# Pairing neighbouring heads, and issuing attention's small fp32 products four in a row on TensorE

## Chip, cores and metric

One core of one Trainium2 chip runs the kernel. The metric is device time in microseconds of one execution. Times of the kernel before are the median of 3 runs and one further execution taken with the profiler.

## What is computed

Attention over `q`, `k`, `v` of 4 batches, 8 heads, 576 positions and 64 features, then two feed-forward layers over the 2304 tokens of 512 features:

```python
q_d, k_d, v_d = (x.reshape(B, H, S // 4, 4, D).mean(axis=3) for x in (q, k, v))
out_d = softmax_attention(q_d, k_d, v_d)          # 144 x 144 scores for each batch and head
out_up = np.repeat(out_d, 4, axis=2)
mask = np.abs(pos[:, None] - pos[None, :]) < 4    # 7 keys for each query
out_local = masked_softmax_attention(q, k, v, mask)
x = (out_up + out_local).transpose(0, 2, 1, 3).reshape(B * S, H * D)
h = x @ w_in                                      # 512 -> 2048
x = (np.maximum(h, 0) + alpha * np.minimum(h, 0)) @ w_out
xn = x / rms(x) * rms_g
g, val = xn @ w_gate, xn @ w_val                  # 512 -> 1536 each
out = (silu(g) * val) @ w_out2
```

## The kernel before, in words

**Dense layers.** Activations and weights are split into a high and a low fp16 half, and each product is three fp16 matmuls (high by high, high by low, low by high). `h_mm` (L1249, tile `hps`) is the product with `w_in`, `o_mm` (L1266, tiles `acc`) that with `w_out`; `m2` holds the second layer: `gps` (L1348) for gate and value, `oacc` (L1377, L1395) for the output. Six blocks of 384 tokens pass through; the first ones run in pieces of 192. The weights arrive as 64-bit words of which `Piece.decode` (L1016) makes fp32 with ScalarE and VectorE; `split` (L345) makes the two halves, one instruction on ScalarE and one on VectorE.

**Attention.** Heads are worked in pairs, as `j` = 0 and 1, that lie on partitions 0 to 63 and 64 to 127. Before, the pair is (h, h+4), so row 64j+d of the tile that goes into the dense layer holds feature d of head h+4j, and `cols` (L967) fetches `w_in` in that order: two transfers of 64 partitions for each half of a piece.

- The pooled attention is `down_tasks` (L561) for batches 1 to 3, and `Dense.down` (L758) for batch 0. For each of 4 pairs it makes 4 fp32 products for the scores (`sps`, L612 and L774) and 4 for the output (`avps`, L651 and L810). A score product takes 64 rows of the array, an output product 64 of its columns, and `j` says which half.
- The local attention of batch 0 is done on TensorE (`Dense.local`, L819) in three chunks `c` of 192 queries and two lanes of two pairs. For each lane and chunk `s1` makes scores (`lsps`): for every pair, half chunk and `j` one mask product (L832, bf16, 102 columns), at the edges of the sequence a product of 3 columns (L835, L837), and the fp32 product of q and k (L839) on top. `s4` makes the output (`lops`, L893), 4 fp32 products for each pair.
- The local attention of batches 1 to 3 (`local_tasks`, L433) runs on GpSimd and VectorE, with (pair, chunk of the sequence) on 128 partitions: partition 32h+c before.

Each fp32 product stands as two records in the trace.

**What sets the order.** At the end `issue_order` (L24) lists all instructions with a table of costs and lags and plays a list scheduler forwards and backwards for 20 rounds; the best order of each engine is written into the program as dependencies. Every engine, the queue of transfers on SP among them, then works in that order. Before, the table charges TensorE at half rate for the first 150 us (`COLD`).

Of the kernel before, what the change touches and what calls it, by code (L numbers as in the profile page):

```python
# [23 lines left out]
def issue_order(tc, nc, rounds=20):  # L24
# [53 lines left out]
    def transfer(o, i):  # L78
        sides = [[c for _, c in a.ap if c > 1] or [1] for a in (o, i)]
        rings = max(x for x in range(1, 17) if not any(s[0] % x for s in sides))  # L80
        n = max(runs(a)[0] for a in (o, i))
        each = 4.0 * min(runs(a)[1] for a in (o, i))
        share = n / 16 * (12.0 + 0.072 * each)
        return max(share, n / rings * (9.0 + 0.042 * each)), max(share, 600.0)

    def cost(k, ins, outs):
# [16 lines left out]
        if e == "DVE":  # L103
            if i.opcode == "Reciprocal":
                return 69 + 6.25 * n
            fast = i.opcode in ("TensorScalarPtr", "TensorCopy") and not any(psum(a) for a in ins)
            fast = fast and len([a for a in ins if free(a) > 1]) < 2
            return 69 + n / (1.92 if fast else 0.96) + 60 * (extra > 0)
# [65 lines left out]
    succs = [[] for _ in count]  # L174
    for k in count:
# [13 lines left out]
    COLD = 150e3  # L189

    def run(P, S, prio, fwd, d):
# [4 lines left out]
        port = 0.0  # L196
        for k in count:
            if not left[k]:
                heapq.heappush(soon[eng[k]], (0.0, k))
        for _ in count:  # L200
# [5 lines left out]
            if fwd and e == "PE" and t <= COLD:  # L206
                real[k] = 2 * d[k] - 2.5
# [27 lines left out]
def kernel(  # L235
# [14 lines left out]
    nc = tc.nc  # L250
# [21 lines left out]
    P_X, P_W, P_H = 13, 14, 15  # L272
    P_N, P_U = 10, 44
# [75 lines left out]
    def setup():  # L349
# [7 lines left out]
        nc.vector.tensor_scalar(out=pidx, in0=pidx, scalar1=NC - 1, scalar2=None, op0=ALU.bitwise_and)  # L357
        nc.vector.tensor_scalar(out=edge[:, 0:1], in0=pidx, scalar1=0, scalar2=NEG, op0=ALU.is_equal, op1=ALU.mult)
        nc.vector.tensor_scalar(out=edge[:, 1:2], in0=pidx, scalar1=NC - 1, scalar2=NEG, op0=ALU.is_equal, op1=ALU.mult)
# [22 lines left out]
    def load_q(g, tag=None):  # L382
# [3 lines left out]
                      ap=[[TT * D, 128], [HP * HS, 2], [1, T * D]])  # L386
# [3 lines left out]
    def load_kv(x, g, tag=None):  # L390
# [5 lines left out]
        def src(p0, n, j0, nj, r0=0, nr=R):  # L396
            return bass.AP(tensor=x.tensor, offset=base + p0 * TT * D + j0 * HP * HS + r0 * D,
                           ap=[[TT * D, n], [HP * HS, nj], [1, nr * D]])

        if b == 0 and t0 == 0:  # L400
            nc.gpsimd.memset(t[0:1, 0, 0:W], 0.0)
            nc.sync.dma_start(out=t[1:113], in_=src(1, 112, 0, 2))
            nc.sync.dma_start(out=t[113:128], in_=src(113, 15, 0, 2))
            nc.sync.dma_start(out=t[0:1, 1:2], in_=src(0, 1, 1, 1))
            nc.sync.dma_start(out=t[0:1, 0:1, W:R], in_=src(0, 1, 0, 1, W, R - W))
        elif b == B - 1 and t0 + T == TT:
            nc.gpsimd.memset(t[96:128, 1, R - W:R], 0.0)
            nc.sync.dma_start(out=t[0:112], in_=src(0, 112, 0, 2))
            nc.sync.dma_start(out=t[112:127], in_=src(112, 15, 0, 2))
            nc.sync.dma_start(out=t[127:128, 0:1], in_=src(127, 1, 0, 1))  # L410
            nc.sync.dma_start(out=t[127:128, 1:2, 0:R - W], in_=src(127, 1, 1, 1, 0, R - W))
        else:
            nc.sync.dma_start(out=t, in_=src(0, 128, 0, 2))
        return t

    def load_sd(x, b, h, tag=None):
        t = rawtile([SH, 2, 2, 4 * D], tag, "sd")
        for j in range(2):
            src = bass.AP(tensor=x.tensor, offset=x.offset + (b * H + h + HP * j) * HS,
# [13 lines left out]
    def local_tasks(g, engs, tags=(None, None, None), av_pool=True, o_at=None):  # L433
# [92 lines left out]
        def trans(half):  # L526
            def f():
# [5 lines left out]
                ps = ps.rearrange("p t (h c r) -> p t h c r", h=HP, r=2)  # L533
# [27 lines left out]
    def down_tasks(b, h, tags=(None, None, None), solo=False):  # L561
# [44 lines left out]
        def smm():  # L606
# [3 lines left out]
            for a in range(2):  # L610
                for j in range(2):
                    nc.tensor.matmul(  # L612
                        ps[j][0:SH, a], t[j * 64:j * 64 + 64, 0, a * SH:(a + 1) * SH],
                        t[j * 64:j * 64 + 64, 1, :], start=True, stop=True)
# [30 lines left out]
        def avm():  # L645
# [3 lines left out]
            for kh in range(2):  # L649
                for j in range(2):  # L650
                    nc.tensor.matmul(ps[j * 64:j * 64 + 64, :], st["pv"][:, kh, j],  # L651
                                     st["aT"][:, j, kh * SD:(kh + 1) * SD], start=(kh == 0), stop=(kh == 1))
# [20 lines left out]
    class Dense:  # L673
# [12 lines left out]
        def load(self, h):  # L686
# [4 lines left out]
            for i, (nm, x) in enumerate((("q", q), ("k", k))):  # L691
                st[nm] = t[0:TP6, i * n:(i + 1) * n]
                for j in range(2):
                    nc.sync.dma_start(
                        out=st[nm].rearrange("p (r j d) -> p r j d", r=R6, j=2)[:, :, j],
                        in_=bass.AP(tensor=x.tensor, offset=x.offset + (self.b * H + h + HP * j) * HS,
                                    ap=[[R6 * D, TP6], [D, R6], [1, D]]))

        def loadv(self, h):
# [4 lines left out]
                in_=bass.AP(tensor=v.tensor, offset=v.offset + (self.b * H + h) * HS,  # L704
                            ap=[[8 * D, SH], [HP * HS, 2], [1, 8 * D]]))

        def vwin(self, h, c):
# [3 lines left out]
            def part(p0, p1, w, nw, j):  # L711
                src = v.offset + (self.b * H + h + HP * j) * HS + (w * QT - W + p0) * D
# [45 lines left out]
        def down(self, h):  # L758
            st = self.st[h]

            def smm():
# [10 lines left out]
                for a in range(2):  # L772
                    for j in range(2):
                        nc.tensor.matmul(  # L774
                            ps[j][0:SH, a], t[j * 64:j * 64 + 64, 0, a * SH:(a + 1) * SH],
                            t[j * 64:j * 64 + 64, 1, :], start=True, stop=True)
# [29 lines left out]
            def avm():  # L806
                ps = ps_t.tile([128, SD], F32, tag="at", name="avps")
                for kh in range(2):
                    for j in range(2):
                        nc.tensor.matmul(ps[j * 64:j * 64 + 64, :], st["pv"][:, j, kh],  # L810
# [798 lines left out]
```

## Time and profile before

| | |
|---|---|
| runs | 1036.86, 1039.5 and 1041.29 us, median 1039.5 |
| profiled execution | 1034.7 us, span 1033.0 us |
| busy, of the span | TensorE 95%, VectorE 68%, ScalarE 49%, GpSimd 14% |
| mean granted TensorE clock | 0.99 |
| chain that ended last | TensorE 73%, VectorE 10%, ScalarE 8%, transfers 5% |

Busy TensorE counts every matmul from its start to its modelled end, and neighbours overlap, so it says that something is under way and not how fast. What a product takes of TensorE is read from the start of one instruction to the start of the next. The clock column knows only what the records of the clock tell; the first of them is at 122.6 us, and until then the column reads 1.00.

### The profile page before, as it was taken

Reading aid. Unit: us, or ns where it says so; the run is one execution under the profiler, and the core shown is the slowest. Engines: PE = TensorE matmul, PEld = TensorE weight load, DVE = VectorE, ACT = ScalarE, POOL = GpSimd, SP = SyncE. Lnnn points to the kernel's source line nnn. Section 1 sums busy time; section 2 is a strip of 40 time slices with the busy share of each in tenths; the row PEclk is TensorE's granted clock in tenths of the full one; section 3 lists DMA queues with packets and bytes.
Section 4 is the critical chain, followed back from the end, with each engine's and each line's share of the span. In section 5 each row is a group of like instructions: output and inputs, shape, how many; then the busy total and the mean of one; then the engine's idle time right before and its main releaser. Section 6 shows DMA issues by size and latency. Waiting matters only on the chain.

```text
span 1033.0 us, 16284 instructions
## 1 busy us (share of the span) xinstructions
PE 977.2 (95%) x6232; PEld 611.1 (59%) x6232; DVE 699.2 (68%) x1483; ACT 506.1 (49%) x1214; POOL 142.1 (14%) x118
## 2 busy tenths in 40 slices
PE   3699989999989999998999999999999999999998
PEld 2465667778966555555666565555556666555554
DVE  1568797899999977999976599994333353352333
ACT  2886898799987465123366532222132242321222
POOL 2422121111201101333200232310000000000000
PEclk9999979999999999999999999999999999999999
DMA  9974543554432133112121021100010000000100
GB/s 173 193 173 142 177 142 101 177 182 140 161 93 92 41 101 105 57 66 70 33 85 60 31 77 47 31 16 16 1 31 2 1 1 1 1 1 1 31 1 31
DMA packets 50008, 74.54 MB, mean 72 GB/s; under 512 B 17718, under 2 KB 30922, under 8 KB 49930
## 3 DMA queue, kind: packets, MB, share of 16 engines
q1 hardware_dynamic: 49930, 73.50, 24.7%
q8 instruction: 49, 0.80, 0.3%
q14 instruction: 29, 0.24, 0.1%
HBM read 68.76 MB, written 4.72 MB: 71 GB/s over the span
## 4 chain that ended last, share of the span: by engine, by line
PE 73%; DVE 10%; ACT 8%; DMA 5%; issue 2%; SPq 1%; POOL 0%; ACTq 0%; DVEq 0%
PE gps L1348 24%; PE hps L1256 15%; PE acc L1269 13%; PE oacc L1377 12%; DMA out_dram<-ob 3%; PE avps L651 2%; ACT sqs L1039 1%; PE lops L893 1%; ACT wr L1020 1%; PE sps L612 1%; DVE ls L460 1%; DVE prod L449 1%; DMA wr<-in_moe_w_in_dram 1%; PE lsps L839 1%; ACT wr L1023 1%
## 5 line engine op out<-in xcount | busy, mean ns | idle before, releaser
L1256 PE MATMUL hps<-xt,wi 128*128 128x192 f16 (+1 forms) x1536 | 359.9, 296 | 4.1 <-DVE g L347 2.8
L1348 PE MATMUL gps<-x,w 128*128 128x384 f16 x1728 | 344.3, 327 | 3.4 <-DVE uhl L1369 1.3
L1269 PE MATMUL acc<-ghl,wo 128*128 128x384 f16 (+1 forms) x960 | 251.6, 311 | 5.4 <-ACT ghl L346 2.7
L1348 PEld LDWEIGHTS <-w 128*128 128x128 f16 x1728 | 169.2, 98 | 117.4 <-issue 6.5
L1377 PE MATMUL oacc<-w,uhl 128*128 128x512 f16 x630 | 192.9, 379 | 1.4 <-ACT ob L1433 1.4
L1256 PEld LDWEIGHTS <-wi 128*128 128x128 f16 x1536 | 153.5, 103 | 68.0 <-issue 16.4
L1269 PEld LDWEIGHTS <-wo 128*128 128x128 f16 x1344 | 128.6, 98 | 69.4 <-issue 8.6
L1262 DVE SCALAR_TENSOR_TENSOR hps<-g,oma,hps 128x192 f32<-128x192 f32 (+1 forms) x128 | 66.1, 517 | 77.9 <-ACT g L1260 77.6
L1357 ACT ACTIVATE th<-gps,tsc 128x384 f32<-128x384 f32 x72 | 41.7, 579 | 143.5 <-PE gps L1348 143.2
L1377 PEld LDWEIGHTS <-uhl 128*128 128x128 f16 x630 | 61.7, 98 | 66.2 <-issue 2.4
L1359 DVE SCALAR_TENSOR_TENSOR th<-th,gps 128x384 f32<-128x384 f32 x72 | 39.6, 550 | 88.4 <-ACT th L1357 88.2
L1260 ACT ACTIVATE g<-hps 128x384 f32<-128x384 f32 x96 | 46.9, 489 | 106.7 <-PE hps L1256 106.6
L1368 ACT ACTIVATE uhl<-gps 128x384 f16<-128x384 f32 x72 | 41.6, 577 | 99.1 <-DVE gps L1362 92.8
L449 POOL TENSOR_TENSOR prod<-cq,ckv 128x896 f32<-128x896 f32 x24 | 52.6, 2194 | 250.3 <-DMA ckv<-in_k_dram 74.2
L1269 PE MATMUL acc<-g,wo 128*128 128x384 f16 (+1 forms) x384 | 67.6, 286 | 1.5 <-ACT x L1283 1.1
L497 POOL TENSOR_TENSOR prod<-ls,ckv 128x896 f32<-128x896 f32 x24 | 45.0, 1875 | 160.8 <-DVE lo L510 60.7
L1369 DVE TENSOR_TENSOR uhl<-gps,uhl 128x384 f16<-128x384 f32 x72 | 45.3, 629 | 30.6 <-ACT uhl L1368 30.4
L510 DVE TENSOR_TENSOR prod<-prod 128x384 f32<-128x384 f32 (+1 forms) x108 | 59.7, 563 | 5.4 <-POOL prod L497 5.4
L346 ACT ACTIVATE ghl<-hps,sc 128x384 f16<-128x384 f32 x72 | 41.7, 579 | 44.2 <-DVE hps L1262 38.4
L347 DVE SCALAR_TENSOR_TENSOR ghl<-hps,sc,ghl 128x384 f16<-128x384 f32 x72 | 44.2, 614 | 25.4 <-ACT ghl L346 25.1
L460 DVE TENSOR_REDUCE ls<-prod 128x14 f32<-128x896 f32 x54 | 57.6, 1075 | 0.0
L1020 ACT ACTIVATE wr<-wr 128x768 f32<-128x768 f32 (+1 forms) x48 | 41.5, 865 | 1.7 <-DMA wr<-in_moe_w_in_dram 1.7
(235 smaller groups left out, 1232.0 us busy)
## 6 DMA issues: line engine op xcount, KB each, us to landing
wr<-in_moe_w_out_dram SPq DMA_DIRECT2D x18, 512.0 KB
wr<-in_moe_w_in_dram SPq DMA_DIRECT2D x20, 384.0 KB
wr<-in_moe_w_gate_dram SPq DMA_DIRECT2D x8, 768.0 KB
wr<-in_moe_w_val_dram SPq DMA_DIRECT2D x8, 768.0 KB
ckv<-in_k_dram SPq DMA_DIRECT2D x7, 768.0 KB
ckv<-in_v_dram SPq DMA_DIRECT2D x7, 768.0 KB
wr<-in_moe_w_out_dram SPq DMA_DIRECT2D x20, 256.0 KB
out_dram<-ob SPq DMA_DIRECT2D x13, 256.0 KB
```

The costliest lines, as they stand in the source:

```text
L449: engs[i].tensor_tensor(out=pr, in0=view(st["q"][:, j, t:t + TP], [[D, TP], [0, ND], [1, D]]), in1=view(st["k"][:, j, t:t + TP], [[D, TP], ...
L460: nc.vector.tensor_reduce(out=st["s"][:, j, t:t + TP], in_=st.pop(("p", i)), axis=AX.X, op=ALU.add)
L497: engs[i].tensor_tensor(out=pr, in0=view(st["s"][:, j, t:t + TP], [[ND, TP], [1, ND], [0, D]]), in1=view(st["v"][:, j, t:t + TP], [[D, TP] ...
L510: add = lambda o, a, c: nc.vector.tensor_tensor(out=o, in0=a, in1=c, op=ALU.add)
L1020: nc.scalar.activation(out=hi.bitcast(F32), in_=hi.bitcast(F32), func=AF.Prelu, scale=2.0 ** -112, alpha=2.0 ** 32)
L1256: nc.tensor.matmul(ps[:, j], wi[:, f + j, a, kk * 128:(kk + 1) * 128], x[:, b_, kk, c0:c0 + n], start=(i == 0), stop=(i == 3 * KK - 1))
L1260: nc.scalar.activation(out=g, in_=ps, func=AF.Relu, scale=-1.0)
L1262: nc.vector.scalar_tensor_tensor(out=ps[:, j], in0=g[:, j], scalar=oma[:, f + j:f + j + 1], in1=ps[:, j], op0=ALU.mult, op1=ALU.add)
L1269: nc.tensor.matmul(acc[e], wo_f(f)[:, a, e * 128:(e + 1) * 128], hl[:, b_], start=(f == 0 and i == 0), stop=(f == NF - 1 and i == 2))
L1348: nc.tensor.matmul(ps, w2_t[i0 + f // 3].rearrange("p a (k c) -> p a k c", k=KK)[:, a, kk, (f % 3) * 128:(f % 3 + 1) * 128], xh[:, b_, kk] ...
L1369: nc.vector.tensor_tensor(out=t1, in0=vp, in1=t0, op=ALU.subtract)
L1377: nc.tensor.matmul(acc[tt], t[:, a, tt * 128:(tt + 1) * 128], w[:, b_, f % 3], start=(f in first and i == 0), stop=(f in last and i == 2))
```

## The change

Heads are paired (2h, 2h+1). Row 64j+d is then feature 128h+64j+d, as `w_in` has it, and a half piece of `w_in` is one transfer to 128 partitions. All loads of `q`, `k` and `v` take the new heads, and the local attention of batches 1 to 3 has partition 4c+h. `load_kv` loses a branch that batch 0 had and cuts its last tile into five transfers in place of four.

In `s1` the mask is written for a whole bank by one product of 408 columns, the edges by products of 2x3, and the fp32 products follow. The four fp32 products of a pair (in `sps`, `avps`, `lsps` and `lops`) are recorded as a group by `together()`. `issue_order` makes the members of a group a chain, lets the first wait for what any of them needs, and puts them on TensorE directly behind each other. Its costs are other ones, and TensorE's rate is now modelled from the work of each stretch.

```diff
-def issue_order(tc, nc, rounds=20):
+def issue_order(tc, nc, groups, rounds=20):
...
-        share = n / 16 * (12.0 + 0.072 * each)
+        share = n / 16 * (10.0 + 0.046 * each)
...
-            if o.ap[0][1] == 64 and o.offset // row(o) == 64:
-                return 22.5
...
-            return n * 2 / 2.4 + 25 if i.is_transpose else n * 4 / 2.4 + 60
+            return n * 2 / 2.4 + 4 if i.is_transpose else n * 4 / 2.4 + 100
...
-                return 69 + 6.25 * n
+                return 89 + 6.25 * n
...
+    mate, joined, fixed = {}, set(), [0.0] * len(insts)
+    for names in groups:
+        g = [at[n] for n in names]
+        for a, b in zip(g, g[1:]):
+            mate[a] = b
+            preds[b].add(a)
+        for a in g:
+            preds[g[0]] |= preds[a].difference(g)
+        joined.update(g)
+        fixed[g[0]] += 100.0
+        fixed[g[-1]] += 145.0
+    for k in joined:
+        dur[k] = free(aps[k][1][0]) * 2 / 2.4 + 2.5
...
-            if fwd and e == "PE" and t <= COLD:
-                real[k] = 2 * d[k] - 2.5
+            if fwd and e == "PE":
+                while t >= (win + 1) * WIN:
+                    slow, win, done = done < BUSY, win + 1, 0
+                done += work[k]
+                real[k] = (2 * d[k] - 2.5 if slow else d[k]) + fixed[k]
...
-                    heapq.heappush(soon[eng[s]], (at[s], s))
+                    if fwd and mate.get(k) == s:
+                        heapq.heappush(now[e], (-1e30, s))
+                    else:
+                        heapq.heappush(soon[eng[s]], (at[s], s))
...
+    groups = []
+
+    @contextmanager
+    def together():
+        n = len(nc.cur_bb.bb.instructions)
+        yield
+        groups.append([i.name for i in nc.cur_bb.bb.instructions[n:]])
...
         src = bass.AP(tensor=q.tensor, offset=q.offset + b * H * HS + t0 * D,
-                      ap=[[TT * D, 128], [HP * HS, 2], [1, T * D]])
+                      ap=[[TT * D, NC], [2 * HS, HP], [HS, 2], [1, T * D]])
...
                 ps = [ps_t.tile([128, 2, SD], F32, tag="at", name="sps") for j in range(2)]
-            for a in range(2):
-                for j in range(2):
-                    nc.tensor.matmul(
+            with together():
+                for a in range(2):
+                    for j in range(2):
+                        nc.tensor.matmul(
...
+                for j in range(2):
+                    nc.tensor.matmul(ps[j][0:QT], identb, view(maskb, [[0, 2], [0, QC], [1, KW]]), start=True, stop=False)
...
-                        for j in range(2):
-                            nc.tensor.matmul(o[j], identb, maskb, start=True, stop=False)
...
+                    with together():
+                        for i in range(QC):
+                            q0 = W + (c * QC + i) * QT
+                            for j in range(2):
+                                nc.tensor.matmul(ps[j][0:QT, n, i], T_[j * 64:j * 64 + 64, 0, q0:q0 + QT],
+                                                 T_[j * 64:j * 64 + 64, 1, q0 - W:q0 + QT + W],
+                                                 start=False, stop=(n == 1 and i == QC - 1))
...
     def cols(w, c0, n, half):
-        if w is w_in:
-            return [(slice(j * D, (j + 1) * D), bass.AP(
-                tensor=w.tensor, offset=w.offset + (HP * j + 2 * half) * D * FF + c0,
-                ap=[[FF, D], [D * FF, 2], [1, n]])) for j in range(2)]
```

The order that results, at three places.

TensorE, in the pooled attention of batch 3 beside the first dense layer (`sps` the scores, `hps` the product with `w_in`). Before:

```order
L1256 MATMUL hps<-xt,wi 128x384
L612 MATMUL sps<-qkT 72x144
L1256 LDWEIGHTS wi
L1256 MATMUL hps<-xt,wi 128x384
L612 MATMUL sps<-qkT 72x144
L1256 LDWEIGHTS wi
L1256 MATMUL hps<-xt,wi 128x384
L612 MATMUL sps<-qkT 72x144
L1256 LDWEIGHTS wi
L1256 MATMUL hps<-xt,wi 128x384
L612 MATMUL sps<-qkT 72x144
```

and with the change:

```order
L1284 LDWEIGHTS wi
L1284 MATMUL hps<-xt,wi 128x384
L640 MATMUL sps<-qkT 72x144 x4
L1284 LDWEIGHTS wi
L1284 MATMUL hps<-xt,wi 128x384
```

Four fp32 products that each stood between two fp16 products are one run of four. In the whole order before, 224 such products stand in 159 runs, 130 of them of one; with the change they stand in 49 runs, 44 of four, three of eight and two of twelve.

TensorE, in the local attention of batch 0 (`lsps` the scores with their mask), last chunk. Before:

```order
L839 MATMUL lsps<-T_203 96x102
L1256 LDWEIGHTS wi
L1256 MATMUL hps<-xt,wi 128x192
L832 LDWEIGHTS maskb
L832 MATMUL lsps<-maskb 96x102
L1256 LDWEIGHTS wi
L1256 MATMUL hps<-xt,wi 128x192
L837 LDWEIGHTS maskb
L837 MATMUL lsps<-maskb 96x3
L1256 LDWEIGHTS wi
L1256 MATMUL hps<-xt,wi 128x192
L839 MATMUL lsps<-T_203 96x102
```

and with the change:

```order
L857 LDWEIGHTS maskb
L857 MATMUL lsps<-maskb 96x408
L1284 LDWEIGHTS wi
L1284 MATMUL hps<-xt,wi 128x192
L861 LDWEIGHTS maskb
L861 MATMUL lsps<-maskb 96x2x3
L1284 LDWEIGHTS wi
L1284 MATMUL hps<-xt,wi 128x192
L869 MATMUL lsps<-T_202 96x102 x4
L1284 LDWEIGHTS wi
L1284 MATMUL hps<-xt,wi 128x192
L869 MATMUL lsps<-T_211 96x102 x4
```

The mask goes first and in one piece, and the fp32 products of a pair follow as one run.

SP, the first transfers (`wo` is the space where q and k of batch 0 land, `wr` the raw weights, `sdv` v). Before:

```order
L694 DMA wo<-in_k_dram 96x6x64
L694 DMA wo<-in_q_dram 96x6x64
L694 DMA wo<-in_k_dram 96x6x64
L1001 DMA wr<-in_moe_w_in_dram 64x2x768
L702 DMA sdv<-in_v_dram 72x2x512
L694 DMA wo<-in_q_dram 96x6x64
L694 DMA wo<-in_k_dram 96x6x64
L1001 DMA wr<-in_moe_w_in_dram 64x2x768
```

and with the change:

```order
L1029 DMA wr<-in_moe_w_in_dram 128x2x768
L723 DMA wo<-in_q_dram 96x6x64
L723 DMA wo<-in_k_dram 96x6x64
L723 DMA wo<-in_q_dram 96x6x64
L1029 DMA wr<-in_moe_w_in_dram 128x2x768
L723 DMA wo<-in_q_dram 96x6x64
L731 DMA sdv<-in_v_dram 72x2x512
L723 DMA wo<-in_k_dram 96x6x64
```

The first weights stand ahead of all of q and k, where ten transfers of q and k stood ahead of them. Ahead of the last k of batch 0 there are now 8 transfers of `w_in` of 768 KB, and there were 13 of 384 KB.

## Rows read from the trace of the kernel before

**Rows 1.** Busy by stretch: length, PE, PEld, DVE, ACT, POOL, PEclk, DMA share, GB/s.

```profile
50.00:102.50 52.50, 48.30 (x242) 31.46 (x239) 40.22 (x96) 41.70 (x143) 11.11 (x10) 1.00 0.63 162
102.50:185.00 82.50, 78.56 (x542) 55.73 (x539) 67.72 (x161) 72.65 (x206) 14.06 (x10) 0.90 0.43 133
185.00:300.00 115.00, 106.42 (x1058) 90.81 (x1056) 109.32 (x238) 100.90 (x195) 19.73 (x9) 0.99 0.49 162
365.00:410.00 45.00, 44.70 (x272) 24.14 (x271) 33.41 (x76) 27.55 (x94) 3.48 (x2) 1.00 0.37 113
535.00:592.00 57.00, 57.00 (x361) 33.47 (x360) 36.11 (x80) 34.35 (x107) 6.20 (x3) 1.00 0.16 51
592.00:1033.00 441.00, 432.90 (x2537) 249.41 (x2535) 225.99 (x427) 125.11 (x238) 28.87 (x18) 1.00 0.06 17
```

**Rows 2.** Timeline of PE, lone products of batch 3: start us, us, engine, line, operation.

```profile
548.06 0.46 PE L651 MATMUL avps<-aT,dd 72*64 72x144 f32 x2
548.45 0.34 PE L1256 MATMUL hps<-xt,wi 128*128 128x384 f16 x1
548.72 0.46 PE L651 MATMUL avps<-aT,dd 72*64 72x144 f32 x2
```

**Rows 3.** Chain that ended last, a stretch of fp16 products alone: start us, us, what.

```profile
885.94 5.85 PE gps L1348 x36
```

**Rows 4.** Timeline of PE, three score products in a row, batch 3.

```profile
551.57 0.34 PE L1269 MATMUL acc<-ghl,wo 128*128 128x384 f16 x1
551.84 0.71 PE L612 MATMUL sps<-qkT 64*72 64x144 f32 x6
552.48 0.82 PE L1269 MATMUL acc<-ghl,wo 128*128 128x384 f16 x4
```

**Rows 5.** Timeline of PE before the first record of the clock: four in a row, and lone ones.

```profile
97.67 1.24 PE L612 MATMUL sps<-qkT 64*72 64x144 f32 x8 [0.56 <-ACT qkT L603]
...
107.12 0.74 PE L651 MATMUL avps<-aT,dd 72*64 72x144 f32 x2
...
108.06 0.74 PE L651 MATMUL avps<-aT,dd 72*64 72x144 f32 x2
```

**Rows 6.** Timeline of PE, output products of the local attention, lone and three in a row.

```profile
136.66 0.38 PE L893 MATMUL lops<-laT,vw 102*64 102x96 f32 x2
...
137.16 0.38 PE L893 MATMUL lops<-laT,vw 102*64 102x96 f32 x2
...
182.37 0.54 PE L893 MATMUL lops<-laT,vw 102*64 102x96 f32 x6
182.92 0.24 PE L1256 MATMUL hps<-xt,wi 128*128 128x192 f16 x1
```

**Rows 7.** Busy PE by stretch, of the tile avps alone.

```profile
20.00:102.50 82.50, 9.35 (x40) 1.00 0.73 173
102.50:185.00 82.50, 7.49 (x24) 0.90 0.43 133
```

**Rows 8.** Busy PE by stretch, of the tile sps.

```profile
20.00:102.50 82.50, 11.89 (x48) 1.00 0.73 173
102.50:185.00 82.50, 4.11 (x16) 0.90 0.43 133
```

**Rows 9.** Busy PE by stretch, of line L839, scores of the local attention.

```profile
20.00:102.50 82.50, 16.77 (x64) 1.00 0.73 173
102.50:185.00 82.50, 7.08 (x32) 0.90 0.43 133
```

**Rows 10.** Busy PE by stretch, of line L893, outputs of the local attention.

```profile
20.00:102.50 82.50, 5.93 (x28) 1.00 0.73 173
102.50:185.00 82.50, 14.17 (x72) 0.90 0.43 133
```

**Rows 11.** Busy time by stretch, a wait of PE and what follows (columns as rows 1).

```profile
292.00:296.00 4.00, 1.33 (x17) 1.18 (x15) 4.00 (x5) 2.74 (x5) 1.42 (x1) 1.00 0.00 0
296.00:300.00 4.00, 3.10 (x15) 1.92 (x15) 3.65 (x8) 4.00 (x7) 0.00 (x0) 0.58 0.00 0
```

More of the change, by code (lines that the diff above doesn't have):

```diff
@@ L2 @@
 from collections import deque
-from contextlib import ExitStack
+from contextlib import ExitStack, contextmanager
 import concourse.bass as bass
@@ L188, in issue_order @@
     engines = sorted(set(eng))
-    COLD = 150e3
+    WIN, BUSY = 3413.0, 2900
+    work = [0 if eng[k] != "PE" or not aps[k][1] else
+            free(aps[k][1][0]) * (1 if wide(aps[k][0][0]) == 2 or insts[k].is_transpose else 2) for k in count]
     def run(P, S, prio, fwd, d):
@@ L196, in run @@
         port = 0.0
+        win, done, slow = 0, 0, True
         for k in count:
@@ L394, in load_kv, with part @@
         base = x.offset + b * H * HS + (t0 - W) * D
[L396 to L406, printed above, removed]
-            nc.gpsimd.memset(t[96:128, 1, R - W:R], 0.0)
[L408 to L411, printed above, removed]
+        def part(c0, nc_, h0=0, nh=HP, j0=0, nj=2, nr=R):
+            p = HP * c0 + h0
+            nc.sync.dma_start(
+                out=t[p:p + (nc_ - 1) * HP + nh, j0:j0 + nj, 0:nr],
+                in_=bass.AP(tensor=x.tensor, offset=base + c0 * TT * D + (2 * h0 + j0) * HS,
+                            ap=[[TT * D, nc_], [2 * HS, nh], [HS, nj], [1, nr * D]]))
+        assert b > 0
+        if b == B - 1 and t0 + T == TT:
+            nc.gpsimd.memset(t[96:128, 1, R - W:R], 0.0)
+            part(0, NC // 2)
+            part(NC // 2, NC // 2 - 1)
+            part(NC - 1, 1, 0, HP - 1)
+            part(NC - 1, 1, HP - 1, 1, 0, 1)
+            part(NC - 1, 1, HP - 1, 1, 1, 1, R - W)
         else:
-            nc.sync.dma_start(out=t, in_=src(0, 128, 0, 2))
+            part(0, NC)
         return t
@@ L648, in avm @@
             ps = ps_t.tile([128, SD], F32, tag="at", name="avps")
[L649 to L652 removed]
+            with together():
+                for kh in range(2):
+                    for j in range(2):
+                        nc.tensor.matmul(ps[j * 64:j * 64 + 64, :], st["pv"][:, kh, j],
+                                         st["aT"][:, j, kh * SD:(kh + 1) * SD], start=(kh == 0), stop=(kh == 1))
             nc.scalar.activation(out=outd_t[b][:, h, :], in_=ps, func=AF.Copy)
@@ L771, in smm @@
                 ps = [pool_of(self.smp[j]).tile([128, 2, SD], F32, tag=self.smp[j], name="sps") for j in range(2)]
[L772 to L776, printed above, removed]
+                with together():
+                    for a in range(2):
+                        for j in range(2):
+                            nc.tensor.matmul(
+                                ps[j][0:SH, a], t[j * 64:j * 64 + 64, 0, a * SH:(a + 1) * SH],
+                                t[j * 64:j * 64 + 64, 1, :], start=True, stop=True)
                 m = att.tile([SH, 2, 2], F32, tag=f"dm{h % 2}", name="dm")
@@ L807, in avm @@
                 ps = ps_t.tile([128, SD], F32, tag="at", name="avps")
-                for kh in range(2):
-                    for j in range(2):
-                        nc.tensor.matmul(ps[j * 64:j * 64 + 64, :], st["pv"][:, j, kh],
-                                         st["aT"][:, j, kh * SD:(kh + 1) * SD], start=(kh == 0), stop=(kh == 1))
+                with together():
+                    for kh in range(2):
+                        for j in range(2):
+                            nc.tensor.matmul(ps[j * 64:j * 64 + 64, :], st["pv"][:, j, kh],
+                                             st["aT"][:, j, kh * SD:(kh + 1) * SD], start=(kh == 0), stop=(kh == 1))
                 if h == 0:
@@ L890, in s4 @@
                     ps = pool_of(banks[n]).tile([128, QC, QT], F32, tag=banks[n], name="lops")
-                    for i in range(QC):
-                        for j in range(2):
-                            nc.tensor.matmul(ps[j * 64:j * 64 + 64, i], st["vw"][:, c * QC + i, j], ls["t"][n][:, i, j],
-                                             start=True, stop=True)
+                    with together():
+                        for i in range(QC):
+                            for j in range(2):
+                                nc.tensor.matmul(ps[j * 64:j * 64 + 64, i], st["vw"][:, c * QC + i, j],
+                                                 ls["t"][n][:, i, j], start=True, stop=True)
                     tag = ("ob", "xs", "ra", "rb")[h]
```

47 lines of the change are left out of this document (21 added, 26 removed).

## The prediction

> **What bounds the kernel now.** I read the busy time by stretch first [rows 1]. TensorE is busy 48.3 of 52.5 us from 50 us on, 78.6 of 82.5 in the next stretch, and all of 57.0 where batch 3's pooled attention runs. But busy is not fast, so the second view is the timeline, where the start-to-start time says what a product takes of the engine. Alone, an fp16 product of 384 columns takes 5.85 / 36 = 0.16 us [rows 3]. An fp32 product of attention that stands between two of them takes more: from one to the next, with one fp16 product between, it is 548.72 - 548.06 = 0.66, so 0.50 for itself [rows 2]. The reader should see where it goes. After the fp32 product's start 0.39 passes until the fp16 product starts, and after that one 0.27 instead of 0.16: some 0.1 us of lead each time the engine goes over to the small product.
>
> The third view is the same timeline where three stand in a row: from the fp16 product before them to the one behind, 552.48 - 551.57 = 0.91, less 0.16, so 0.75 for three [rows 4]. Three cost half as much again as one. That is the whole case for the change.
>
> **What the change takes away, part by part.** Counts are records halved, as each product has two.
>
> *Batches 2 and 3 (365 to 410 and 535 to 592).* Each has four pairs with 4 score and 4 output products. The 16 output products of a batch stand alone: 16 x 0.50 = 8.0. The scores stand as 1 + 3 in all pairs of batch 2: 4 x (0.50 + 0.75) = 5.0; in batch 3 in three pairs, one pair is four lone ones: 3.75 + 2.0 = 5.75. Together 26.75 us. A group of four is not shown at this rate. It cannot be less than the 0.75 of three, and not more than that plus the mean of the second and third, (0.75 - 0.50) / 2 = 0.13, so 0.75 to 0.88; I take 0.80, since the two values of j start together in the rows of four and of three [rows 4, 5]. 16 groups cost 12.8. **Gain 14.0** (12.7 to 14.75). All of it is on the path: TensorE is busy throughout there, and VectorE has 11.6 of 45 and 20.9 of 57 us idle [rows 1].
>
> [...]
>
> *102.5 to 185.* Busy time of the lone products is 7.49 + 4.11 + 7.08 + 14.17 = 32.85 us for 144 records, 72 products [rows 7 to 10]. A lone one takes 0.04 more than its busy time (0.50 against 0.46 [rows 2]; an output of the local attention 137.16 - 136.66 less 0.08, half of the 0.16, for the fp16 product of 192 columns is 0.42 against 0.38 [rows 6]), so 32.85 + 72 x 0.04 = 35.7. As groups: 5 of the kinds sps and avps at 0.80. For the 13 of the local attention, three in a row take 182.92 - 182.37 = 0.55 and the lead of 0.1, so 0.65 [rows 6]; a fourth makes it 0.65 to 0.75, I take 0.70. Together 4.0 + 9.1 = 13.1, **22.6 us less of TensorE's time**. How much is on the path? Here VectorE and ScalarE are nearly full too: up to 300 us VectorE has 14.8 + 5.7 = 20.5 us idle, ScalarE 9.9 + 14.1 = 24.0 [rows 1], and what they do there (decoding and splitting `w_out` and the second layer's weights) must be done before the second layer can run. So the stretch can't shrink by more than 20.5 unless work moves out of it, and some of that idle time lies between dependent steps. I take three quarters: **gain 15** (0 to 22.6).
>
> *Before 102.5.* 9.35 + 11.89 + 16.77 + 5.93 = 43.9 us busy for 180 records, some 88 products when those on the border are counted once [rows 7 to 10]. [...] Four in a row last 1.24 [rows 5], and a lone one takes 108.06 - 107.12 - 0.16 = 0.78. Of 22 groups, 11 cost 1.24 and 11 of the local attention 0.70 x 0.78 / 0.50 = 1.09: 25.6 us, so TensorE's work falls by some 18. It is no longer the only bound here: from 50 us on ScalarE has 10.8 and VectorE 12.3 us idle [rows 1]. I take half: **gain 9** (0 to 10.8).
>
> *Nothing* I charge for the rest. The mask: 48 products of 102 columns become 12 of 408, the same columns. `w_in` brings the same bytes in 12 transfers fewer. That the last k of batch 0 now stands behind 8 x 768 KB in place of 13 x 384 KB is 1.2 MB more ahead of it, at the 162 GB/s of [rows 1] 7 us; the cover is TensorE's queue of 50 to 102 us, in which the heads that come last wait behind other attention work; without it the 7 us would eat most of the 9. In return the first weights land first, and ScalarE and VectorE, which have little to do then, start earlier. A group waits for the last operand of four, and the fp16 products behind it wait too; the scheduler puts the group where all of them are there, and if it errs, the operand it misses is one ScalarE copy, under 1 us for each of 56 groups, inside the ranges above.
>
> Sum: 14 + 15 + 9 = 38 us. The profiled execution, 1034.7, goes to 996.7. The median of the runs is 4.8 above it, and measured as a median I expect 1039.5 - 38 = **1001.5 us, say 1001**.
>
> **The rivals.**
>
> *All of TensorE's relief passes through.* 14.0 + 22.6 + 18 = 55: 984 us. For it: TensorE is the busiest engine in every stretch, and the scheduler can move VectorE's later work behind 365 us, where it idles. Against it: VectorE at 109.3 of 115 [rows 1]. Chance 0.15.
>
> *The first 300 us don't shrink.* VectorE and ScalarE bind there, TensorE only waits more, and 14 remains: 1026 us. For it the same row; against it the 20.5 idle microseconds. Chance 0.17.
>
> *Slower, by the clock.* [...] Chance 0.04.
> [...]
>
> *The change doesn't do what it says:* four in a row cost what four lone ones do, 1039. Rows 4 and 5 speak against it: chance 0.04.
>
> **How the numbers follow.** The forecast has 0.60, its own range 985 to 1015, from the bounds of its three terms. I leave out the slower case, that of no effect, and the ends of the first two rivals: **976 to 1026**. A measurement can tell about 0.5% from no change, 5 us; the first three cases are faster by more: **faster 0.92, same 0.04, slower 0.04**.
>
> **What would show it.** Right: in batches 2 and 3 each run of eight records takes 0.75 to 0.88 us with its lead, and the two stretches are 14 us shorter together. Of the first 300 us some 24 are gone, with VectorE near full from 100 us on. Everything after 592 keeps its 441 us [rows 1]: nothing there changes. Wrong: groups that start late with TensorE idle before them; VectorE idle as much as before with TensorE waiting, which would mean an order worse than the old one; or a granted clock well under 0.97 from 185 to 300.

## The result, and the profile after

| | before | changed |
|---|---|---|
| median of four runs | 1040.14 us | 1010.68 us |
| profiled execution, span | 1034.7, 1033.0 us | 1012.3, 1010.6 us |
| TensorE busy, of the span | 977.2 us, 95% | 930.8 us, 92% |
| mean granted clock | 0.990 | 0.981 |

The change is faster: ratio 0.9711, 95% interval 0.9671 to 0.9752, some 30 us. One of the changed kernel's four runs, 1022.8 us, was slow: it stands in the median and not in the ratio, and without it the median is 1009.05 us. The two profiled executions lie 22.4 apart. The one before ran 5.4 under its median, the one after 1.6 over its own, so differences read from these two traces come out up to 7 us too small.

The stretches of [rows 1], now of the changed kernel (same columns):

```profile
50.00:102.50 52.50, 35.20 (x231) 25.07 (x227) 46.67 (x98) 41.58 (x146) 12.62 (x7) 1.00 0.62 187
102.50:185.00 82.50, 59.11 (x535) 50.05 (x534) 71.96 (x159) 71.48 (x187) 19.05 (x12) 0.83 0.41 135
185.00:300.00 115.00, 113.10 (x1092) 94.83 (x1091) 107.53 (x250) 103.23 (x203) 11.49 (x6) 0.99 0.45 142
365.00:410.00 45.00, 44.01 (x286) 25.36 (x285) 34.39 (x66) 18.60 (x59) 10.39 (x5) 1.00 0.32 105
535.00:592.00 57.00, 57.00 (x383) 35.39 (x383) 47.56 (x87) 26.03 (x74) 14.43 (x7) 1.00 0.24 78
```

Until 185 us TensorE is no longer full: it was busy 78.56 of 82.5 from 102.5 us on, now 59.11. From 185 us on it is full again.

The timeline of TensorE, a group of four scores in batch 2, answers to [rows 4], one of outputs to [rows 2], and a group of the local attention to [rows 5] and [rows 6] (before 100 us, ahead of the first record of the clock):

```profile
356.98 0.65 PE L1376 MATMUL gps<-x,w 128*128 128x384 f16 x3
357.56 0.71 PE L640 MATMUL sps<-qkT 64*72 64x144 f32 x8
358.21 0.34 PE L1376 MATMUL gps<-x,w 128*128 128x384 f16 x1
...
365.70 0.71 PE L680 MATMUL avps<-aT,dd 72*64 72x144 f32 x8
366.35 0.28 PE L627 MATMUL qkps<-ident,qkp 72*128 72x72 f32 x1
...
67.73 1.00 PE L869 MATMUL lsps<-T 64*96 64x102 f32 x8
68.66 0.38 PE L627 MATMUL qkps<-ident,qkp 72*128 72x72 f32 x1
```

From the group's start to the next product 358.21 - 357.56 = 0.65. The three fp16 products ahead take 0.58 where 3 x 0.16 = 0.48 is theirs, so 0.10 of lead, and a group of four costs 0.75. A lone product took 0.39 by its starts [rows 2], and four of them now take 0.65. The group of the local attention takes 0.93 there by its starts.

To see where time came and went, I count the fp16 products (5256 in every kernel, as many of each kind) by their starts on TensorE, and note when the one starts that has k of them before it. This is a clock of progress, and the small products hardly disturb it: at the 300th, those of the pooled attention of batches 0 and 1 and of the local attention are all done in both kernels.

| profiled execution | first | 300th | 450th | 1200th | 2000th | 3000th |
|---|---|---|---|---|---|---|
| before | 102.7 | 184.7 | 203.6 | 283.1 | 439.0 | 630.7 |
| changed | 98.3 | 164.8 | 196.8 | 276.6 | 419.7 | 606.6 |
| gained | 4.4 | 19.9 | 6.8 | 6.5 | 19.3 | 24.1 |

So 20 us were there at the 300th product and 13 of them were lost over the next 150. How they were lost is read in three views of the stretch around it. First busy time, before and then after (columns as [rows 1]):

```profile
122.50:153.00 30.50, 27.37 (x185) 19.53 (x183) 28.30 (x55) 28.77 (x67) 8.22 (x5) 0.78 0.56 183
153.00:185.00 32.00, 31.19 (x261) 23.56 (x261) 23.69 (x70) 27.66 (x85) 3.37 (x4) 0.94 0.34 96
```

```profile
122.50:153.00 30.50, 23.20 (x237) 19.12 (x238) 28.20 (x64) 21.57 (x68) 7.61 (x8) 0.89 0.26 90
153.00:185.00 32.00, 21.01 (x178) 18.59 (x176) 28.78 (x60) 31.14 (x67) 7.00 (x4) 0.77 0.64 215
```

Then what TensorE waited for from 153 to 185 us in the changed kernel (us in total, times, longest), and the two longest waits of the issuing queue of the transfers from 102.5 to 153 us:

```profile
PE hps L1284 <- DVE g L376: 6.5, 3, 5.0
PE allps L349 <- ACT sqs L1067: 4.5, 1, 4.5
```

```profile
SPq L1039 <- DVE wo L1053: 29.4, 2, 18.6
SPq L1039 <- DVE hps L1290: 3.8, 1, 3.8
```

TensorE waits 11 of 32 us, on VectorE and ScalarE; ScalarE is busy 31.14 of 32 with decoding and squaring `w_out` (lines 1048, 1051, 1067). Until 153 us ScalarE had room (21.57 of 30.5 us, 28.77 in the kernel before) and the transfers stood at 0.26 of their time (0.56 before), while the loads of `w_out` waited for raw buffers that VectorE's decoding gives back. And the products behind the longest of these waits were slow. The rows of the timeline ahead of it and behind it:

```profile
163.86 2.14 PE L1284 MATMUL hps<-xt,wi 128*128 128x192 f16 x24 [0.83 <-DVE g L376]
170.99 6.98 PE L1284 MATMUL hps<-xt,wi 128*128 128x192 f16 x48 [4.99 <-DVE g L376]
```

Behind it 48 products of 192 columns take 0.145 us each, ahead of it 24 of the same take 0.09, and a product of twice the columns takes 0.16 alone [rows 3]. The granted clock of the stretch is 0.77, and 0.51 from 171 to 177 us. The kernel before had such a stretch too, 0.78 from 122.5 to 153 us; from 102.5 to 185 us the mean fell from 0.90 to 0.83.

### The profile page after: what moved, and what is told of

Read it like the earlier page. It is cut to its first block, busy times and chain, and to the rows that moved or that the text cites. A ratio compares the mean times of both kernels' runs of the same rounds, so it can differ in the third digit from the quotient of the medians.

```text
span 1010.6 us, 16163 instructions
## 1 busy us (share of the span) xinstructions
PE 930.8 (92%) x6188; PEld 594.4 (59%) x6188; DVE 702.7 (70%) x1482; ACT 506.8 (50%) x1214; POOL 147.8 (15%) x118
## 4 chain that ended last, share of the span: by engine, by line
PE 71%; ACT 11%; DVE 8%; DMA 6%; issue 3%; SPq 1%; POOL 1%; ACTq 0%; POOLq 0%; DVEq 0%
PE gps L1376 22%; PE acc L1297 17%; PE hps L1284 14%; PE oacc L1405 11%; DMA out_dram<-ob 3%; ACT sqs L1067 1%; ACT wr L1048 1%; DVE prod L537 1%; ACT wr L1051 1%; DMA sdv<-in_v_dram 1%; PE lsps L869 1%; SPq L723 1%; ACT dls L889 1%; DMA wr<-in_moe_w_out_dram 1%; PE avps L680 1%
## 5 line engine op out<-in xcount | busy, mean ns | idle before, releaser
L1284 PE MATMUL hps<-xt,wi 128*128 128x192 f16 (+1 forms) x1536 | 336.4, 296 | 9.9 <-DVE g L376 8.2
L1284 PEld LDWEIGHTS <-wi 128*128 128x128 f16 x1536 | 151.0, 103 | 66.8 <-issue 17.0
L476 POOL TENSOR_TENSOR prod<-cq,ckv 128x896 f32<-128x896 f32 x24 | 55.1, 2297 | 211.6 <-DVE ghl L376 56.7
L537 DVE TENSOR_TENSOR prod<-prod 128x384 f32<-128x384 f32 (+1 forms) x108 | 62.5, 590 | 3.1 <-POOL prod L524 3.1
L1297 PE MATMUL acc<-g,wo 128*128 128x384 f16 (+1 forms) x384 | 61.9, 286 | 0.7 <-ACT wo L375 0.5
```

The lines of the kernel that those rows point to most:

```text
L476: engs[i].tensor_tensor(out=pr, in0=view(st["q"][:, j, t:t + TP], [[D, TP], [0, ND], [1, D]]), in1=view(st["k"][:, j, t:t + TP], [[D, TP], ...
L537: add = lambda o, a, c: nc.vector.tensor_tensor(out=o, in0=a, in1=c, op=ALU.add)
L1284: nc.tensor.matmul(ps[:, j], wi[:, f + j, a, kk * 128:(kk + 1) * 128], x[:, b_, kk, c0:c0 + n], start=(i == 0), stop=(i == 3 * KK - 1))
L1297: nc.tensor.matmul(acc[e], wo_f(f)[:, a, e * 128:(e + 1) * 128], hl[:, b_], start=(f == 0 and i == 0), stop=(f == NF - 1 and i == 2))
```

## The experiments

Ratios are to the kernel before, timed on the same chip; where medians and ratios say different things about two kernels, I give both. The changed kernel and e6 differ only in two neighbours' places within 24 groups, and their 2000th and 3000th products lie 2.9 and 4.3 us apart. So I read nothing into differences under 5 us in the table.

| run | median, us | ratio, interval | 300th | 450th | 1200th | 2000th | 3000th |
|---|---|---|---|---|---|---|---|
| changed | 1010.68 | 0.9711 (0.9671 to 0.9752) | 164.8 | 196.8 | 276.6 | 419.7 | 606.6 |
| e1 groups given up | 1038.34 | 1.0004 (0.9981 to 1.0028) | 184.1 | 203.3 | 288.6 | 438.5 | 632.6 |
| e2 old pairs | 1024.76 | 0.9877 (0.9844 to 0.9910) | 176.3 | 208.4 | 294.2 | 438.1 | 625.5 |
| e3 old prices | 1008.62 | 0.9717 (0.9689 to 0.9745) | 169.9 | 192.2 | 273.8 | 416.1 | 601.2 |
| e4 groups from batch 1 on | 1014.37 | 0.9770 (0.9746 to 0.9793) | 176.6 | 196.4 | 275.8 | 424.9 | 609.2 |
| e5 short squares | 1009.96 | 0.9723 (0.9693 to 0.9752) | 164.8 | 196.0 | 276.5 | 419.1 | 605.9 |
| e6 order in the group | 1013.38 | 0.9757 (0.9718 to 0.9797) | 162.8 | 195.0 | 274.6 | 416.8 | 602.3 |
| e7 short VectorE work | 1008.57 | 0.9710 (0.9666 to 0.9755) | 162.4 | 194.0 | 274.1 | 416.3 | 603.2 |
| e8 both short | 1005.79 | 0.9674 (0.9628 to 0.9720) | 161.0 | 192.0 | 273.1 | 416.3 | 602.0 |
| e9 short squares, free order | 1009.99 | 0.9718 (0.9687 to 0.9749) | 167.6 | 186.4 | 267.2 | 419.7 | 605.6 |
| e10 short VectorE, free order | 1006.28 | 0.9696 (0.9661 to 0.9730) | 179.0 | 198.3 | 275.7 | 418.6 | 603.1 |
| e11 merged squares | 1007.45 | 0.9699 (0.9673 to 0.9725) | 159.3 | 188.7 | 277.4 | 419.2 | 604.5 |
| e12 merged, old prices | 1009.36 | 0.9719 (0.9694 to 0.9745) | 168.2 | 190.0 | 270.6 | 414.9 | 603.5 |

**What made the gain: e1 to e4.** The change has four parts that can be undone alone: the groups, the pairing, the table of prices, and where the groups are.

e1:
```
-    issue_order(tc, nc, groups)
+    issue_order(tc, nc, [])
```


> The changed kernel with its groups given up: the planner gets no list, so it may put fp16 products between the members again and prices them singly; pairing of heads, transfers, masks and the new cost table stay. Theory (adjacency is the gain): the tiled products of batches 2 and 3, 12.2 us in the changed kernel, go back to about 25 us and those of the first 185 us cost at least 5 us more on the path, so 1025 to 1040 us. Rival (the new table and the pairing made the gain): 1005 to 1016 us, with batches 2 and 3 still near 12 us.

All of the gain is gone; adjacency it is. In batch 3 the output products stand alone again:

```profile
550.65 0.46 PE L680 MATMUL avps<-aT,dd 72*64 72x144 f32 x2
551.04 0.34 PE L1284 MATMUL hps<-xt,wi 128*128 128x384 f16 x1
551.31 0.46 PE L680 MATMUL avps<-aT,dd 72*64 72x144 f32 x2
```

From the starts in the timeline, the tiled products of batches 2 and 3 take 10.7 + 11.2 = 21.9 us again (before 21.3, changed 10.7), and they stand in 48 separate runs (before 50, changed 16); with 0.1 of lead for each this is the difference that was expected. The pairing and the prices alone bring nothing.

e2, the loads, the edge masks of batches 1 to 3 and the transposes of before put back, of which `w_in`'s:
```
     def cols(w, c0, n, half):
+        if w is w_in:
+            return [(slice(j * D, (j + 1) * D), bass.AP(
+                tensor=w.tensor, offset=w.offset + (HP * j + 2 * half) * D * FF + c0,
+                ap=[[FF, D], [D * FF, 2], [1, n]])) for j in range(2)]
```


> The changed kernel with heads paired (h, h+4) and w_in in twice as many transfers over 64 partitions each, as before; groups, masks and table stay. Theory (the pairing only feeds the first 100 us, where the first hps product came 4.5 us earlier): 1011 to 1018 us, with all of the difference before 105 us. Rival (the pairing does nothing that lasts, since 13 of the 20 us gained by 165 us were lost again by 190 us): within 2 us of the changed kernel. Second rival (the transfers of w_in held the queue for the loads behind them): over 1020 us.

The second rival by its number: 14 us slower than the changed kernel by the medians, 17 by the ratios, all of it before the 1200th product, the first product at 113.5 us in place of 98.3. Busy time by stretch of e2 and of the changed kernel (last column GB/s), and the longest pieces of e2's chain up to 75 us (start us, us, what):

```profile
0.00:20.00 20.00, 7.25 (x38) 4.99 (x38) 1.24 (x11) 5.61 (x10) 6.13 (x32) 1.00 0.93 169
20.00:50.00 30.00, 11.90 (x65) 8.75 (x66) 12.94 (x33) 21.88 (x69) 12.16 (x14) 1.00 1.07 178
```

```profile
0.00:20.00 20.00, 5.81 (x30) 4.16 (x30) 5.69 (x16) 9.30 (x19) 6.59 (x32) 1.00 1.02 252
20.00:50.00 30.00, 20.72 (x122) 14.35 (x121) 17.74 (x48) 28.90 (x94) 16.43 (x21) 1.00 0.89 241
```

```profile
13.05 12.22 DMA wr<-in_moe_w_in_dram
25.29 11.94 DMA wr<-in_moe_w_in_dram
37.24 11.06 DMA wo<-in_q_dram
51.17 9.83 DMA wr<-in_moe_w_in_dram
61.02 10.72 DMA wr<-in_moe_w_in_dram
```

The transfer engines are about as busy, but move 169 and 178 GB/s where `w_in` goes to 64 partitions at a time, and 252 and 241 where it goes to 128. The order of the transfers doesn't explain it: the kernel before moves 168 and 191 in these stretches, and e1, e3 and e4, which all have the wide transfers in plans of their own, 213 to 275. The rows differ 1.35 to 1.5 times, as an average over all transfers of the stretch. A narrow transfer is also half as large (384 KB against 768), and that was not separated. The kernel before has the same narrow transfers and its first product at 102.7, so part of the 14 us may lie in the plan of e2, whose new price for transfers counts on more speed than the transfers to 64 partitions had here. That share was not separated either.

e3, the former prices:
```
-        share = n / 16 * (10.0 + 0.046 * each)
+        share = n / 16 * (12.0 + 0.072 * each)
...
-            return n * 2 / 2.4 + 4 if i.is_transpose else n * 4 / 2.4 + 100
+            return n * 2 / 2.4 + 25 if i.is_transpose else n * 4 / 2.4 + 60
...
-                return 89 + 6.25 * n
+                return 69 + 6.25 * n
...
-                real[k] = (2 * d[k] - 2.5 if slow else d[k]) + fixed[k]
+                real[k] = (2 * d[k] - 2.5 if t <= 150e3 else d[k]) + fixed[k]
```


> The changed kernel with the planner's former prices (DMA share, 69 ns on VectorE, 60 and 25 ns on TensorE, double times up to 150 us) and the groups kept. Theory (the table only shuffles the first 300 us): 1003 to 1020 us, batches 2 and 3 still near 12 us. Rival (the table is what let the groups pay early): 1020 to 1030 us, with the index of the 200th fp16 product back by over 8 us.

In the time as the theory had it: the table of prices changes nothing that can be measured. The rival's other sign did come, and meant nothing for the end: the 200th product starts at 154.6 us in place of 145.0, 9.6 later, and at the 450th e3 is already 4.6 us ahead.

e4, in the class for batch 0, at four places:
```
-                with together():
+                if True:
```


> The changed kernel with groups only in batches 1 to 3 (the sps and avps of the functions for those batches); the four places of batch 0 are planned singly. Theory (early groups pay on the path by about 8 us of the 17 that the changed kernel gained before 300 us, late ones by 13): 1015 to 1025 us. Rival A (what the early groups gain is given back before 190 us to ScalarE and the late loads of w_out): 1009 to 1013 us. Rival B (early groups carry more than the late): over 1026 us.

Between the theory and rival A, 1014.4 us. That is 3.7 us above the changed kernel by the medians and 6 by the ratios, whose intervals just overlap: batch 0's groups are worth some 4 to 6 us of the end, if that. Yet they take much off TensorE, as the busy time of e4 shows:

```profile
0.00:102.50 102.50, 76.31 (x338) 48.30 (x338) 64.74 (x163) 80.63 (x257) 33.27 (x58) 1.00 0.82 217
102.50:185.00 82.50, 73.19 (x559) 56.01 (x559) 67.98 (x157) 68.29 (x185) 16.41 (x12) 0.88 0.38 116
```

Together 149.5 us, against 120.8 in the changed kernel up to 185 us: 28.7 us less of TensorE, and the 450th product starts at 196.4 and 196.8. The groups of batches 1 to 3 carry 1038.3 - 1014.4 = 24 us.

**How a group of four gets cheap: e6.** The middle two change places in the groups of batches 1 to 3; they are swapped in the finished plan, so the rest of it is kept:
```
-                for a in range(2):
-                    for j in range(2):
+                for j in range(2):
+                    for a in range(2):
```


> In batches 1 to 3 the two middle products of each group of four change places, so that the two of one half of the rows follow each other (j outer); everything else keeps its place and its time in the plan. Theory (neighbours on different tile positions run side by side, so that a group of four is two spans of some 0.32 us and a lead): three spans, 0.32 us more per group, 5 us for the 16 groups of batches 2 and 3, so 1015 to 1018 us with records of these groups at 1.0 to 1.1 us in place of 0.75. Rival (the gain is only that the array is entered and left once for four products): no change, 0.75 us a group and within 2 us of the changed kernel.

The theory falls by its number: 0.65 us as before, 1013.4 us, an interval that overlaps. The timeline of TensorE in e6:

```profile
354.64 0.72 PE L651 MATMUL sps<-qkT 64*72 64x144 f32 x8
355.29 0.50 PE L1387 MATMUL gps<-x,w 128*128 128x384 f16 x2
```

But neither is the rival's picture right. The eight records of such a group (two a product) start at these distances, in ns:

```
changed  7 173  7 116  7 116  7 215
e6      14 166 14 109 13 110 13 215
before, one alone 180 215; three 7 173 7 116 123 215
```

They still come in pairs. Two records on one half of the rows start 122 to 180 ns apart in the changed kernel and the one before, so I take the pair at 14 ns for the first product and the third, which works on the other half though the second stands ahead of it. The waits for semaphores bear this out. Two of the eight weight loads of a score group carry one: the first two in seven of the eight score groups of batches 2 and 3, and in the one that ran out of step (345.30 us) the first and the fifth, which is the third product's. So, by these distances, a group is four pairs of records in either order: 4 x 0.12, and some 0.15 beyond that, 0.64 in all (0.65 measured). A lone product has two records and the same 0.15, 0.39 and the lead (180 + 215 ns measured).

**What gave the early gain back: e5, e7, e8.** Here the order is kept as in the changed kernel, by letting the planner count the shortened work in full.

e5, for `w_out` (the first line is the planner's):
```
+        n = full.get(i.name, n)
...
-                    src, o = self.c[:, i * DM:(i + 1) * DM], sqs
+                    c = slice(i * DM, (i + 1) * DM) if self.w is not w_out else slice(i * DM + DM // 2 - 4, i * DM + DM // 2 + 4)
+                    src = self.c[:, c]
+                    o = sqs[:, 0:src.shape[1]]
...
+                if self.w is w_out:
+                    full[nc.cur_bb.bb.instructions[-1].name] = DM
```


> The squares of w_out on ScalarE read 8 columns each in place of 512 (so the sum of squares, and with it w_out's scale, is left out in the main); the planner still counts them at full length, so that the order stays that of the changed kernel. 14 of the 16 lie between 122.5 and 185 us at 0.63 us; shortened they should save some 7 us of ScalarE there. Theory (ScalarE, busy 31.1 of 32 us from 153 to 185, is what gave back 13 of the 20 us gained by 165 us): 4 to 7 us faster than the changed kernel, 1004 to 1007 us, and the 400th fp16 product by 4 us or more earlier. Rival (VectorE, 28.8 of 32 us there): under 2 us. Second rival (the late w_out transfers): under 1 us.

e7, for block 3:
```
-            nc.vector.tensor_reduce(out=st["s"][:, j, t:t + TP], in_=st.pop(("p", i)), axis=AX.X, op=ALU.add)
+            pr = st.pop(("p", i))
+            nc.vector.tensor_reduce(out=st["s"][:, j, t:t + TP], in_=pr[:, :, :, 0:8] if g == 3 else pr, axis=AX.X, op=ALU.add)
...
-                add(pr[:, :, 0:3], pr[:, :, 0:3], pr[:, :, 3:6])
...
+                pc = pr[:, :, :, 0:8] if g == 3 else pr
+                add(pc[:, :, 0:3], pc[:, :, 0:3], pc[:, :, 3:6])
...
```


> In block 3's attention the six reductions of q times k and the twelve first adds of the products with v work on 8 of 64 columns on VectorE (most of these sums is left out); the planner counts them in full, so the order stays. Between 122.5 and 185 us that takes 8 adds of 0.77 us and 4 reductions of 1.07 us down to some 0.2 us, about 8 us of VectorE. Theory (ScalarE sets that stretch): under 2 us faster than the changed kernel. Rival (VectorE sets it): 4 to 8 us faster, 1003 to 1007 us.

e8 has both edits.


> Both of the shortenings before in one kernel, order kept. If ScalarE alone sets the stretch: as with the short squares alone, within 2 us. If the two take turns: more than the sum of both alone, 8 to 14 us under the changed kernel. If neither sets it (late transfers of w_out): within 3 us of the changed kernel.

My theory that ScalarE alone sets the stretch is refuted. Busy time of e5 and of e8 there:

```profile
153.00:185.00 32.00, 21.60 (x186) 19.16 (x186) 29.89 (x62) 27.57 (x71) 7.64 (x5) 0.77 0.69 228
```

```profile
153.00:185.00 32.00, 20.70 (x191) 18.40 (x190) 30.80 (x61) 28.30 (x73) 6.26 (x3) 0.84 0.67 219
```

ScalarE is 3.6 us lighter in e5, and the 450th product comes 0.8 us earlier. The chain shows why. Its longest pieces from 157 to 182 us, in the changed kernel and in e5:

```profile
158.38 0.90 ACT wr L1051
160.91 0.92 ACT wr L1051
165.17 1.12 ACT wr L1048 x2
168.02 0.98 ACT wr L1051
169.81 0.94 ACT g L375 x2
```

```profile
165.01 1.28 ACT wr L1049 x2
167.98 1.04 ACT wr L1052
171.63 2.60 DVE wc L1054
176.15 1.07 DVE ls L488
177.22 1.45 DVE wc L1054
```

With ScalarE lighter the chain crosses to VectorE (2.60 on a decoding step, behind which attention's reductions stand), and TensorE waits about as long (10.4 us in place of 11.0). VectorE alone lighter (e7) brought 2.1 us by the medians and nothing by the ratios, both together (e8) 4.9 and 4, all with intervals that overlap the changed kernel's. None of the three cases on record for e8 came clearly, and the 8 to 14 us of two engines that take turns did not come at all. What sets this stretch stays open.

**With a free order: e9, e10.** The same short work, counted short by the planner.
```
-        n = full.get(i.name, n)
```


> The short squares of w_out (8 of 512 columns, the sum left out in the main) with the planner now counting them as short, so that the order is free to use ScalarE's room. With the order kept, ScalarE's 3.6 us less between 153 and 185 us brought nothing. Theory (VectorE's work, 249.6 us of the first 300, is the limit, ScalarE is only late in a kept order): within 3 us of the changed kernel at the 1200th fp16 product, 1007 to 1012 us. Rival (ScalarE's work is the limit and the kept order hid it): 5 us or more earlier there, under 1006 us.

> Block 3's short reductions and adds (8 of 64 columns, most of these sums left out) with the planner counting them as short. With the order kept VectorE had 5.3 us less to do in the first 300 us and the 1200th fp16 product came 2.5 us earlier. Theory (VectorE's work is the limit): the free order brings at least VectorE's 5.3 us by that product, 271 us or less there, and 1001 to 1006 us in all. Rival (the limit is elsewhere): 274 to 279 us there and 1007 to 1012 us.

e9 shows what one look at an index can hide. At the 450th product it is 10 us ahead of the changed kernel, at the 1200th 9, by which its rival would be right; at the 2000th it is level, and the time is the same, as its theory had it. Busy time from 300 us on, of the changed kernel and of e9, and the two longest of TensorE's waits in e9 from 267 to 420 us:

```profile
300.00:340.00 40.00, 39.49 (x236) 23.47 (x235) 38.60 (x97) 23.32 (x47) 5.64 (x3) 1.00 0.10 34
340.00:365.00 25.00, 24.84 (x162) 14.27 (x162) 24.89 (x65) 16.38 (x53) 0.00 (x0) 1.00 0.29 90
```

```profile
300.00:340.00 40.00, 37.69 (x219) 22.48 (x218) 39.01 (x99) 22.64 (x44) 5.83 (x3) 0.96 0.11 37
340.00:365.00 25.00, 24.13 (x164) 13.70 (x162) 24.38 (x66) 16.44 (x54) 0.00 (x0) 1.00 0.32 100
```

```profile
PE oacc L1409 <- ACT x L1315: 2.8, 1, 2.8
PE gps L1380 <- DVE th L1391: 2.4, 2, 2.1
```

VectorE is near full in both and has done 313.1 and 313.5 us of work by 365 us; by then TensorE has started 1728 and 1724 fp16 products. It can be early at 270 us, but not at 365. That fits VectorE's amount of work as the limit, but doesn't show it: TensorE is as full from 300 us on in the changed kernel, and its longest wait in e9 is for ScalarE. And e10 speaks against it. It took 7.1 us of work from VectorE in the first 300 us and reached the 1200th product at 275.7, where the theory wanted 271 or less and the rival 274 to 279; it ended 4.4 us lower by the medians, 2 by the ratios, within the overlap of the intervals.

**Tried as a better version: e11, e12.** Squares of `w_out` and of the second `w_out` over two blocks at once, with the accumulator read once for both; e12 adds e3's prices.
```
+                o = sqs.bitcast(mybir.dt.float8e4)
+                for i, (a, e) in enumerate(((0, 2 * DM), (2 * DM, 3 * DM))[:acc.shape[1]]):
+                    e = min(e, self.nf * DM)
+                    nc.scalar.activation(out=o[:, 0:e - a], in_=self.c[:, a:e], func=AF.Square, accum_out=acc[:, i:i + 1],
+                                         saturate=False)
+                return
...
```


> The squares of w_out and of the second w_out taken two rows of blocks at a time (11 and 8 instructions in place of 16 and 12, the whole sum computed), planned anew. Nine instructions less with their accumulator reads, some 0.4 us each, take 3.6 us off ScalarE. Theory (VectorE is the limit): within 3 us of the changed kernel, 1007 to 1014 us. Rival (ScalarE is): 3 to 6 us faster, 1004 to 1007 us.

> The merged squares together with the planner's former prices, the two edits that keep the whole computation and stood even with the changed kernel or better. Theory (both only shuffle the first 300 us): 1003 to 1012 us. Rival (the two gains add, 2 us of the table and 3.6 of ScalarE): 1003 to 1005 us, which would beat both kernels.

1007.5 and 1009.4 us, 3.2 and 1.3 below the changed kernel's median; by the ratios e11 is 1 below and e12 1 above, with overlapping intervals. Both are where their theories had them, and neither can be told from the changed kernel.

Earlier loads of `w_out` into other raw buffers, which would use the transfer time left before 153 us (the transfers stand at 0.26 there), were not tried. That the late loads squeeze the decoding into 153 to 190 us is read from the waits and remains argued.

## Why the prediction was right, and where it was off

The forecast was 1001 us with a range of 976 to 1026; 1010.7 came. The direction and the cause (adjacency, e1) were right, and the sum of 38 us was 8 too large.

*Batches 2 and 3, 14.0 us: held.* A group costs 0.75, the lower end of 0.75 to 0.88, in place of the 0.80 taken. The tiled products fall from 21.3 to 10.7 us by their starts, and 34 entries fewer at 0.1 are 3.4: together 14.0. From the 1400th to the 3000th product it is 311.4 to 630.7 before and 298.5 to 606.6 after, 11.2 us less, and 12.8 less than in e1. My reading of three in a row as the floor was right.

*102.5 to 185, 15 of 22.6 us, and before 102.5, 9 of 18: the step that failed.* TensorE's own relief was sized well: until 185 us the tiled products were busy 76.8 us before [rows 7 to 10], and 40.8 us in the changed kernel (tiles avps and sps, lines L869 and L925), 36 less where 22.6 + 18 = 41 were forecast. But the two terms promised 24 us on the path, and at the 1400th product 12.9 have arrived in the traces. The step "I take three quarters" went wrong, and "I take half" with it. Both rested on idle microseconds of VectorE and ScalarE summed over long stretches. Those were there, yet not where the work was: ScalarE had 8.9 of 30.5 us free up to 153 us and 0.9 of 32 after it. And I reckoned with the clock only for the rival: TensorE waited 11 us from 153 to 185, and 48 products behind the longest wait took 0.145 us each, where 24 ahead of it took 0.09. e4 gives the sharpest size: of 28.7 us less TensorE work before 185 us, some 4 to 6 reached the end. Which engine or transfer holds TensorE there stays open (e5 to e10).

*Nothing for `w_in`: wrong by reason.* I counted the same bytes in fewer transfers and looked for harm in their order. e2 shows that the transfers to 128 partitions, twice as large, are a gain, 241 to 252 against 169 to 178 GB/s, without which the groups bring half (15 us). It sits inside the early terms, which would have come out smaller still. That the sum came so near is in part luck: an early relief taken too large and a gain taken as nothing offset each other.

*The rivals.* That all passes through (984) is excluded. That the first 300 us don't shrink (1026) came half true. The slower clock never ruled: 0.99 from 185 to 300 us, as before, though 0.77 in one stretch ahead of it. Of the signs named, groups at 0.75 came, and an unchanged end: from the 3000th product to the end of the span 402 us before and 404 now. VectorE near full came only from 122.5 us on. Until 153 us it was so before too (28.20 and 28.30 of 30.5); new is 28.78 of 32 after that, where it had 23.69, and with it TensorE waits.

## What to carry to other kernels

Read what a small product costs from start to start, with its neighbours, and put the products of both halves of the array into one run; their order in it made no difference here (0.65 us a group in both). This part of the forecast held. Where an engine is relieved that shares its stretch with two others nearly as full, don't take a share of the idle time of the whole stretch: look in short windows (30 us here) at which engine is full when the relieved one wants to go on, and ask whether what it gains early can still be kept at the end of that crowd. And judge an experiment at more than one point of progress, since a lead of 9 us at one product was gone 800 products later.

## What the runs showed that I had not expected

In 14 of the 16 groups of batches 2 and 3 a product on one half of the array starts 12 to 15 ns after one on the other half, even where another product of the first half stands between them in the program (e6).

The pairing of heads, which looks like bookkeeping, decides about half of the gain, with e2's plan as it came (e1 and e2: neither the groups without it nor it without the groups give more than 15 of the 30 us).
